# AdaLN block with attention and MLP on one core: fills moved to VectorE, one weight load moved to ScalarE's queue, the first quad planned by due time in pieces of two products

## The chip, the cores and the metric

The kernel runs on 1 core of one Trainium2 chip. The metric is device time in microseconds (us), median of several runs. One further execution was recorded by the hardware profiler; every row quoted below is from it. TensorE is written PE, its weight loads PEld, VectorE DVE, ScalarE ACT, GpSimd POOL, SyncE SP.

## The reference

All inputs are bf16. x is 2048 tokens by 512; there are 32 heads of 16; the MLP is 1376 wide.

```python
mod = (_silu(c) @ w_mod).reshape(c.shape[0], 6, 1, -1)
sa, ca, ga, sb, cb, gb = (mod[:, i] for i in range(6))
h = _layernorm(x) * (1 + ca) + sa
x = x + ga * attention(h, A_wqkv, A_wo)      # softmax(q k^T / 4) v, then wo
h = _layernorm(x) * (1 + cb) + sb
x = x + gb * (gelu(h @ B_w1 + B_b1) @ B_w2 + B_b2)
```

## The kernel before, in words

**Tiles.** The tokens are cut into 4 blocks of 512 (`xb[0..3]`). The normalized, modulated input is held transposed as `hT` (4 chunks of 128 features by 2048 tokens), the keys as `kT`, the values as `VE` (16 key tiles of 128, per head 16 values and two columns of ones, so that the product of weights and `VE` gives numerator and denominator in one). Attention goes by *quads*: one quad is 4 heads (one parity of one chunk of 128 features) for one block of 512 queries; there are 32 quads, each with 16 key tiles. An *item* is one head's scores for one key tile (128x512).

**Two ways to the exponential.** Most items go through ACT: `qk` writes 3 items into PSUM tile `sA`, then 2 into `sB`, in turn, and ACT writes `pA` or `pB` (L967). The key tiles in `DKT` (3, 7, 11, 15) are done by DVE instead: a pass per item turns the scores into int16 `t` whose bits read as f16 are the exponential (L1033, 4 passes for a key tile), and three shifts add a constant (L1054) to give copies that go with scaled values `VV`; four copies are accumulated (`NV = 4`). Quad 0 has no DVE tile in the kernel before, so it gives ACT 64 items and every other quad 48. `do_pv` accumulates into PSUM tile `od` (L1110); the copy `o_sb` (L1142) ends a quad.

**The front.** SP issues the loads in this order: `xb[0]` in four pieces, `W_m0` (1 MB, the modulation weights of the first layer norm), `W_k`, `xb[1]`, `W_q`, `W_v`, `xb[2]`, `xb[3]`, `W_m1`, `W_m2` and the eight pieces of `W_o_pad`. POOL fills `W_o_pad` with zeros (L145) and writes the ones columns of `VE` and `VV` (L142, L143, 56 small memsets). DVE takes the statistics of block 0 (L191), the silu of c (L177 to L179), the root by Newton steps (L196 to L210) and the norm (L216); PE computes the modulation (`psm`, L230), transposes (L221), and projects the first keys and queries (L266, L280); the evacuations are L261, L258, L272, L289 and L287.

**The planner.** From there on a planner in the kernel's Python text runs a clock with estimated durations and writes out a fixed order for each engine. Everything that is not attention is a `Job` with a due time `at` (measured in quads), a list of rows (engine, estimated duration, function), labels that it needs, and `hold`: up to that row it keeps one of two PSUM banks (tiles `aux`). The DVE passes take their scores through the same two banks. `job_for` gives an engine the first ready row of the list of active jobs, and then the first startable job. If PE has nothing ready, `do_fill` issues four products of zeros (L1131). The early jobs (norms, transposes `h_job`, `k_job`, `v_job` of blocks 1 to 3) stand sorted before all others, and until they are done and `end_early` has exchanged the banks, no DVE tile may start (`psd` is empty):

```python
        if not psd and all(o.at >= 0.9 for o in jobs) and not [o for o in active if o.hold >= 0]:
            if all(t + SEM <= clock for t in bank_rel):
                end_early()
```

A projection of four products (`proj_job`), an up-projection (`up_`) and half of an output projection (`oproj`) are one row of PE each, which nothing interrupts. `fill_stream` may hand a late DVE tile back to ACT.

After quad 31 `last_tail` does output projection and MLP of the last block, and `general_path` is a branch for inputs out of range that is not taken.

Of the kernel before, what the change touches and what calls it, by code (L numbers as in the profile page):

```python
# [20 lines left out]
P = 128  # L21
# [3 lines left out]
H = 32  # L25
# [31 lines left out]
EXP = {1: 0.5, 2: 0.92, 3: 1.34}  # L57

# [23 lines left out]
def adaln_block(ctx: ExitStack, tc: tile.TileContext, A_x, A_wqkv, A_wo, B_x, B_w1, B_b1, B_w2, B_b2,  # L82
# [41 lines left out]
    W_m0 = load_mod(0, nc.sync)  # L124
# [16 lines left out]
    def ve_ones(dst, v):  # L141
        nc.gpsimd.memset(dst[:, 0:H * HS].rearrange("p (h e) -> p h e", e=HS)[:, :, 16:HS], v)  # L142
        nc.gpsimd.memset(dst[:, H * HS:VEW], 0.0)  # L143

    nc.gpsimd.memset(W_o_pad, 0.0)  # L145
# [16 lines left out]
    for kt in range(NKT):  # L162
        ve_ones(VE[:, kt, :], 1.0)
    if ndk:
        for i in range(ndk):
            for j in range(1, NV):
                ve_ones(VV[:, i, j - 1, :], WJ[j])
# [25 lines left out]
    def ln_rstd(st, n):  # L193
        mv = small.tile([P, 12, 2], FP32, name="mv")
# [7 lines left out]
        nc.vector.tensor_tensor(out=ri[:, 0:n], in0=magic[:, 0:n], in1=ri[:, 0:n], op=ALU.subtract)  # L202
        r = ri[:, 0:n].bitcast(FP32)
# [30 lines left out]
    def mod_row(ps, W, col0):  # L234
        for j in range(NC):
            nc.tensor.matmul(out=ps, lhsT=scb[:, j, :], rhs=W[:, j, col0:col0 + D],
                             start=(j == 0), stop=(j == NC - 1))
# [26 lines left out]
    def k_proj(ps, ch, b):  # L264
        for j in range(NC):
            nc.tensor.matmul(out=ps, lhsT=W_k[:, j, ch * P:(ch + 1) * P], rhs=hT[:, j, b * 512:(b + 1) * 512],  # L266
                             start=(j == 0), stop=(j == NC - 1))
# [10 lines left out]
    def q_proj(ps, ch, b):  # L278
        for j in range(NC):
            nc.tensor.matmul(out=ps, lhsT=W_q[:, j, ch * P:(ch + 1) * P], rhs=hT[:, j, b * 512:(b + 1) * 512],  # L280
                             start=(j == 0), stop=(j == NC - 1))
# [11 lines left out]
    def v_proj(ps, kt):  # L293
        for j in range(NC):
            nc.tensor.matmul(out=ps, lhsT=hT[:, j, kt * P:(kt + 1) * P], rhs=W_v[:, j, :],  # L295
                             start=(j == 0), stop=(j == NC - 1))
# [33 lines left out]
    with tc.tile_pool(name="pps", bufs=1, space=PSUM) as pps0, \  # L330
# [3 lines left out]
        silu_c()  # L334
        psm = pps0.tile([P, 16], FP32, name="psm")
        first_mod_mm(psm)
        ln1_norm([0], st0)
# [15 lines left out]
    for r in range(4):  # L353
        for par in range(2):
            nc.sync.dma_start(out=W_o4[32 * r:32 * r + 16, :, par, :], in_=wo_v[r][:, :, par, :])
# [15 lines left out]
    early = ExitStack()  # L371
    banks = [early.enter_context(tc.tile_pool(name=f"psE{i}", bufs=1, space=PSUM)) for i in range(2)]
    psd = {}

    def end_early():
        early.close()
        psd["D"] = True
        banks[:] = [att.enter_context(tc.tile_pool(name=f"psX{i}", bufs=1, space=PSUM)) for i in range(2)]
# [26 lines left out]
    def ln_rows(b, src_of, dst_of, key):  # L405
# [3 lines left out]
        def rstd(j):  # L409
            st_of[b] = ln_rstd(st_of[b], 4)  # L410
        rows.append((DVE_, 2.2, rstd))
# [7 lines left out]
    def proj_job(at, mm, evac, needs, label, eng=DVE_, dur=V_EVAC, mms=4):  # L419
        def f(j):  # L420
            j.ps = j.alloc()
            mm(j.ps)

        def g(j):
            evac(j.ps)
        job(at, [(PE_, mms * MM, f), (eng, dur, g)], needs, label, 1)

    def v_job(at, kt):
        eng = V_ENG[kt]
        proj_job(at, lambda ps: v_proj(ps, kt), lambda ps: v_evac(ps, kt, eng), [("h", kt // 4)], ("v", kt),  # L430
                 ACT_ if eng == "act" else DVE_, 0.5 if eng == "act" else V_EVAC)

    def k_job(at, ch, b):
        proj_job(at, lambda ps: k_proj(ps, ch, b), lambda ps: k_evac(ps, ch, b), [("h", b)], ("k", ch, b))

    def q_job(at, ch, b, needs=()):
        proj_job(at, lambda ps: q_proj(ps, ch, b), lambda ps: q_evac(ps, ch, b), [("h", b), *needs],
# [14 lines left out]
    for b in range(1, NQB):  # L452
        at = 0.25 * (b - 1)
        if b > 1:
            def stats(j, b=b):
                st_of[b] = ln1([b])
            job(at - 0.16, [(DVE_, 2.5, stats)], [("n", b - 1)], ("st", b))
# [4 lines left out]
        if b == 1:  # L462
            for kt in range(4):
                v_job(-1.0, kt)
    for kt in range(4, NKT):
        v_job(0.25 * (kt // 4) + 0.04 * (kt % 4), kt)
    n_early = len(jobs)
    jobs.sort(key=lambda o: o.at)
    for i, kt in enumerate(DKT):
        def vv(j, kt=kt):  # L470
            vv_scale(kt)
        job(0.9 + 0.1 * i, [(DVE_, 0.9, vv)], [("v", kt)], ("vv", kt))
    for ch in range(1, NC):
        for b in range(NQB):
            k_job(1.0 + 2 * (ch - 1) * 0.9 + 0.2 * b, ch, b)
        q_job(1.7 + 2 * (ch - 1) * 0.9, ch, 0)

# [10 lines left out]
    def row_job(at, dst, W, col0, label):  # L488
        proj_job(at, lambda ps: mod_row(ps, W, col0), lambda ps: nc.vector.tensor_copy(out=dst, in_=ps),
# [43 lines left out]
    def tail_jobs(b):  # L533
# [15 lines left out]
        def oproj(tt):  # L549
            def f(half):  # L550
                def g(j):
                    if half == 0:
                        j.ps = j.alloc()
                    for t in range(4 * half, 4 * half + 4):
# [11 lines left out]
            def stats(j):  # L566
                ln_stats(T["x1"], T["st"], tt, tt)
            job(p0 + 0.5 + 0.25 * tt, [(PE_, 4 * MM, f(0)), (PE_, 4 * MM, f(1)), (DVE_, V_EVAC, mul),
                                       (POOL_, 1.2, res), (DVE_, V_EVAC, stats)],
                [("begin", b)] + [("ot", b, t) for t in range(8)] + ([("o", b, tt - 2)] if tt > 1 else []),  # L570
                ("o", b, tt), 2)
# [19 lines left out]
        def up_(fc):  # L591
            def f(j):
                j.ps = j.alloc()
                for c in range(NC):
                    nc.tensor.matmul(out=j.ps, lhsT=late["W_1"][:, c, fc * P:(fc + 1) * P], rhs=T["h2"][:, c, :],  # L595
                                     start=(c == 0), stop=(c == NC - 1))

            def g(j):
                nc.vector.tensor_scalar(out=T["u"][:, fc, :], in0=j.ps, scalar1=late["b1c"][:, fc:fc + 1],  # L599
                                        scalar2=None, op0=ALU.add)  # L600
            job(p0 + 2.3 + 0.2 * fc, [(PE_, 4 * MM, f), (DVE_, V_EVAC + 0.05, g)], [("h2", b, c) for c in range(NC)],
                ("u", b, fc), 1)
# [9 lines left out]
        def down(tt):  # L612
            def f(part):
                def g(j):
# [3 lines left out]
                    for fc in range(4 * part, min(NFC, 4 * part + 4)):  # L618
# [8 lines left out]
            def res(j):  # L627
# [3 lines left out]
            job(p0 + 4.9 + 0.5 * tt, [(PE_, 5 * MM, f(0)), (PE_, 4 * MM, f(1)), (PE_, 3 * MM, f(2)),  # L631
                                      (DVE_, V_EVAC, mul), (POOL_, 1.2, res)],
                [("g", b)] + [("y", b, tt - 1)] * (tt > 0), ("y", b, tt) if tt < 3 else ("tail", b), 3)
# [6 lines left out]
    jobs[n_early:] = sorted(jobs[n_early:], key=lambda o: o.at)  # L640
# [233 lines left out]
    def d_of(qi):  # L874
        return DKT if qi > 0 else ()
# [115 lines left out]
    def d_ready():  # L991
        if not psd or not d_tiles or len(d_items) == D_BANKS:
            return False
        if not any(seen_by(t) for t in bank_rel):
# [36 lines left out]
    def do_pass():  # L1031
# [5 lines left out]
        d_prog[0] = qi + (DKT.index(kt) + (4 - len(d_rows_left[(qi, kt)])) / 4) / len(DKT)  # L1037
# [148 lines left out]
    def start_ok(o, eng):  # L1186
        if o.at > progress() or o.rows[0][0] != eng or not all(has(x) for x in o.needs):
            return False
        if o.hold >= 0:
            if psd and any(a.hold >= 0 and a.i <= a.hold for a in active):  # L1190
# [4 lines left out]
    def job_for(eng):  # L1195

        for o in active:
            if o.rows[o.i][0] == eng:
                same = o.i and o.rows[o.i - 1][0] == eng
                if (o.same if same else o.other) <= clock + 1e-6:  # L1200
                    return o
        for o in jobs[:24]:
            if start_ok(o, eng):
                return o
        return None
# [85 lines left out]
    def dve_step():  # L1291
# [6 lines left out]
        if o is not None and (not psd or o.i or d_prog[0] > progress() + 0.1 or o.at + 0.4 < progress()  # L1298
# [28 lines left out]
    while pv["q"] < nq or od_copy or jobs or active:  # L1327
# [6 lines left out]
        if not psd and all(o.at >= 0.9 for o in jobs) and not [o for o in active if o.hold >= 0]:  # L1334
            if all(t + SEM <= clock for t in bank_rel):
                end_early()
                bank_rel[:] = [0.0, 0.0]
# [42 lines left out]
```

## Time and profile before

| | us |
|---|---|
| median of 3 runs | 849.57 (846.89, 849.81, 849.57) |
| the profiled execution, whole | 845.99 |
| its span (first to last instruction) | 844.2 |
| first exponential on ACT starts | 20.05 |
| copy of quad 0, of quad 1 (L1142) starts | 65.53, 99.16 |
| busy: PE, DVE, ACT, POOL | 789.4, 730.8, 755.5, 80.6 |

The page gives busy times per engine, the span in 40 slices, the chain of work that ended last, and groups of instructions by source line. Besides it a trace can be asked for the timeline of a stretch, for who waited for whom, and for the busy time of each engine in given windows. Rows of one line that follow each other are merged ("x4" is four instructions); in square brackets stands the idle time of the engine before the row and what ended it. PE's rows overlap since products are pipelined: the distance between starts counts, not the row's length. What is busy on an engine that others do not wait for costs nothing.

### The profile page before, as it was taken

Reading aid. Unit: us, or ns where it says so; the run is one execution under the profiler, and the core shown is the slowest. Engines: PE = TensorE matmul, PEld = TensorE weight load, DVE = VectorE, ACT = ScalarE, POOL = GpSimd, SP = SyncE. Lnnn points to the kernel's source line nnn. Section 1 sums busy time; section 2 is a strip of 40 time slices with the busy share of each in tenths; the row PEclk is TensorE's granted clock in tenths of the full one; section 3 lists DMA queues with packets and bytes.
Section 4 is the critical chain, followed back from the end, with each engine's and each line's share of the span. In section 5 each row is a group of like instructions: output and inputs, shape, how many; then the busy total and the mean of one; then the engine's idle time right before and its main releaser. Section 6 shows DMA issues by size and latency. Waiting matters only on the chain.

```text
span 844.2 us, 19140 instructions
## 1 busy us (share of the span) xinstructions
PE 789.4 (94%) x7859; PEld 253.0 (30%) x7921; DVE 730.8 (87%) x1306; ACT 755.5 (89%) x672; POOL 80.6 (10%) x125
## 2 busy tenths in 40 slices
PE   3999999999999999999999999999999999999967
PEld 2332322322223222222323223222223222322343
DVE  8747999999988999889989999889987999778573
ACT  2789799999999999999999999989998999999832
POOL 3000000000012000011011000011012000011010
PEclk9999999999999999999999999999999999999989
DMA  9200000004100000000100000000100000000000
GB/s 296 54 1 14 3 16 16 14 16 149 39 15 15 15 16 14 10 21 27 40 14 15 16 14 15 9 21 27 40 15 15 14 16 14 9 21 28 15 26 28
DMA packets 29631, 24.56 MB, mean 29 GB/s; under 512 B 13825, under 2 KB 23394, under 8 KB 29538
## 3 DMA queue, kind: packets, MB, share of 16 engines
q1 hardware_dynamic: 29010, 23.28, 9.4%
q8 instruction: 64, 1.05, 0.5%
q14 instruction: 29, 0.24, 0.1%
q10 hardware_dynamic: 528, 0.00, 0.0%
HBM read 20.65 MB, written 2.61 MB: 28 GB/s over the span
## 4 chain that ended last, share of the span: by engine, by line
PE 43%; DVE 29%; ACT 19%; issue 8%; POOL 1%; DMA 0%; SPq 0%; DVEq 0%; POOLq 0%; ACTq 0%
DVE t L1033 11%; PE od L1110 11%; ACT pA L967 10%; DVE t L1054 9%; ACT pB L967 6%; PE sA L915 5%; PE sB L915 5%; PE od L1131 3%; PE aux L915 3%; PE aux L619 3%; PE aux L595 2%; PE aux L555 2%; PE aux L295 2%; PE aux L266 1%; ACT uG L608 1%
## 5 line engine op out<-in xcount | busy, mean ns | idle before, releaser
L967 ACT ACTIVATE pA<-sA 128x1536 bf16<-128x1536 f32 (+1 forms) x311 | 464.0, 1492 | 25.4 <-PE sA L915 9.7
L967 ACT ACTIVATE pB<-sB 128x1024 bf16<-128x1024 f32 x310 | 330.6, 1067 | 10.3 <-PE aux L915 4.6
L1033 DVE TENSOR_SCALAR t<-aux 128x512 int16<-128x512 f32 x496 | 324.3, 681 | 14.0 <-PE aux L915 12.8
L1054 DVE TENSOR_SCALAR t<-t 128x2048 int16<-128x2048 int16 x372 | 263.9, 728 | 5.5 <-PE od L1110 4.6
L915 PE MATMUL aux<-qm,kT 32*128 32x512 bf16 x496 | 177.4, 380 | 5.7 <-DVE t L1033 4.3
L915 PEld LDWEIGHTS <-kT 32*128 32x128 bf16 x2048 | 77.7, 91 | 260.2 <-issue 254.6
L1110 PE MATMUL od<-pA,VE 128*32 128x512 bf16 x932 | 144.3, 385 | 0.1
L1110 PE MATMUL od<-pB,VE 128*32 128x512 bf16 x620 | 143.2, 385 | 1.0 <-DVE o_sb L1142 0.9
L1110 PE MATMUL od<-t,VV 128*32 128x512 f16 x1488 | 138.3, 384 | 2.5 <-DVE t L1054 2.3
L915 PE MATMUL sA<-qm,kT 32*128 32x512 bf16 x932 | 124.8, 383 | 9.8 <-ACT pA L967 6.7
L915 PE MATMUL sB<-qm,kT 32*128 32x512 bf16 x620 | 122.8, 384 | 1.6 <-ACT pB L967 0.9
L1131 PE MATMUL od<-hT,zeros 128*32 128x512 bf16 x1288 | 108.4, 383 | 0.0
L1167 POOL TENSOR_TENSOR OT<-o_sb,rb 128x512 bf16<-128x512 f32 x31 | 41.6, 1343 | 526.8 <-DMA rb<-d 262.7
L1110 PEld LDWEIGHTS <-VE 128*32 128x32 bf16 x2048 | 50.4, 94 | 101.6 <-issue 89.7
L1110 PEld LDWEIGHTS <-VV 128*32 128x32 bf16 x1488 | 41.0, 95 | 53.3 <-issue 41.4
L1110 PE MATMUL od<-t,VE 128*32 128x512 f16 x496 | 48.4, 384 | 1.0 <-DVE o_sb L1142 1.0
L1131 PEld LDWEIGHTS <-zeros 128*32 128x32 bf16 x1404 | 32.8, 95 | 53.0 <-issue 42.1
L595 PE MATMUL aux<-h2T,W 128*128 128x512 bf16 x114 | 32.9, 382 | 1.5 <-DVE uG L599 0.5
L619 PE MATMUL aux<-W,uG 128*128 128x512 bf16 x121 | 32.2, 387 | 1.7 <-issue 1.6
L1142 DVE COPY o_sb<-od 128x512 f32<-128x512 f32 x32 | 21.9, 685 | 12.2 <-issue 10.7
L599 DVE TENSOR_SCALAR uG<-aux,b1c 128x512 bf16<-128x512 f32 x33 | 24.6, 747 | 4.9 <-PE aux L595 4.7
L555 PE MATMUL aux<-W_o_pad,OT 128*128 128x512 bf16 x88 | 24.1, 382 | 0.6 <-issue 0.3
(126 smaller groups left out, 433.2 us busy)
## 6 DMA issues: line engine op xcount, KB each, us to landing
rb<-d SPq DMA_DIRECT2D x124, 64.0 KB
W_m<-in_w_mod_dram SPq DMA_DIRECT2D x3, 1024.0 KB
xr<-in_A_x_dram SPq DMA_DIRECT2D x4, 512.0 KB
out_dram<-ob SPq DMA_DIRECT2D x16, 128.0 KB
xb<-in_A_x_dram SPq DMA_DIRECT2D x3, 512.0 KB
W<-in_B_w_dram SPq DMA_DIRECT2D x1, 1376.0 KB
W<-in_B_w_dram SPq DMA_DIRECT2D x1, 1280.0 KB
xb<-in_A_x_dram SPq DMA_DIRECT2D x4, 128.0 KB
```

Source lines behind the costliest of these rows:

```text
L555: nc.tensor.matmul(out=j.ps, lhsT=OT[(b, t)][:, tt * P:(tt + 1) * P], rhs=W_o_pad[:, t, :], start=(t == 0), stop=(t == 7))
L595: nc.tensor.matmul(out=j.ps, lhsT=late["W_1"][:, c, fc * P:(fc + 1) * P], rhs=T["h2"][:, c, :], start=(c == 0), stop=(c == NC - 1))
L599: nc.vector.tensor_scalar(out=T["u"][:, fc, :], in0=j.ps, scalar1=late["b1c"][:, fc:fc + 1], scalar2=None, op0=ALU.add)
L619: nc.tensor.matmul(out=j.ps, lhsT=T["u"][:, fc, tt * P:(tt + 1) * P], rhs=late["W_2"][:, fc, :], start=False, stop=(fc == NFC - 1))
L915: nc.tensor.matmul(out=dst, lhsT=kT[32 * r:32 * r + 32, ch, kt * P:(kt + 1) * P], rhs=qm[(b, ch)][32 * r:32 * r + 32, par, :], start=True, ...
L967: nc.scalar.activation(out=pt[:, 0:n, :], in_=st[:, 0:n, :], func=ACT.Exp, scale=math.log(2.0) / STEP)
L1033: nc.vector.tensor_scalar(out=t0[(qi, kt)][:, r, :], in0=sd, scalar1=T_BIAS, scalar2=0.0, op0=ALU.add, op1=ALU.max)
L1054: nc.vector.tensor_scalar(out=t16, in0=t0[(qi, kt)], scalar1=float(MJ[j]), scalar2=None, op0=ALU.add)
L1110: nc.tensor.matmul(out=od[qi][32 * r:32 * r + 32, :], lhsT=w, rhs=src, start=first, stop=last_)
L1131: nc.tensor.matmul(out=dst[32 * r:32 * r + 32, :], lhsT=zeros, rhs=hT[:, r, 0:512], start=bank is not None, stop=bank is not None)
L1142: nc.vector.tensor_copy(out=o, in_=od[qi])
L1167: nc.gpsimd.tensor_tensor(out=OT[(b, t)], in0=o, in1=j.rb, op=ALU.mult)
```

## The change

- **Fills.** POOL's 56 memsets and its fill of `W_o_pad` go. DVE writes the ones columns of all of `VE` in two memsets and of `VV` in six; `warm` (128x512 zeros) is a ninth. `W_o_pad` is zeroed by DVE and loaded by SP in a job `load_wo` at 4.5 quads.
- **W_m0** is issued from ACT's queue, after `cc_bf`.
- **Warm-up.** PE does 18 products of zeros before the modulation and 4 after it.
- **Pieces of two products.** Projections, up, down and output projections are PE rows of two products; between two pieces other work may be issued while the job keeps its bank.
- **Planning of the first quad.** The separate early banks and the gate `psd` go. `job_for` takes the row with the smallest `at` among active and waiting jobs. Statistics become four rows, the root two; `v_job` times change. While progress is below 0.95, DVE takes jobs ahead of passes, and several jobs may hold banks; while it is below 1.0, a DVE tile's row needs both banks free.
- **One DVE tile in quad 0** (`DKT0 = (15,)`): it gives ACT 60 items, DVE 4 passes and 3 shifts.

```diff
+EARLY = 0.95
+D_ALONE = 1.0
+DKT0 = (15,)
...
-    W_m0 = load_mod(0, nc.sync)
+    W_m0 = load_mod(0, nc.scalar)
...
-    nc.gpsimd.memset(W_o_pad, 0.0)
...
-    for kt in range(NKT):
-        ve_ones(VE[:, kt, :], 1.0)
...
+    warm = prow.tile([P, 512], BF16, name="warm")
+    nc.vector.memset(warm, 0.0)
+
+    def ve_ones(dst, v):
+        nc.vector.memset(dst[:, :, 0:H * HS].rearrange("p k (h e) -> p k h e", e=HS)[:, :, :, 16:HS], v)
+        nc.vector.memset(dst[:, :, H * HS:VEW], 0.0)
+
+    ve_ones(VE, 1.0)
+    for j in range(1, NV):
+        ve_ones(VV[:, :, j - 1, :], WJ[j])
...
+        idle = ppsm.tile([P, 512], FP32, name="ppj")
+
+        def warm_up(n):
+            for _ in range(n):
+                nc.tensor.matmul(out=idle, lhsT=warm[:, 0:P], rhs=warm, start=True, stop=True)
+        warm_up(18)
         psm = pps0.tile([P, 16], FP32, name="psm")
         first_mod_mm(psm)
+        warm_up(4)
...
-    for r in range(4):
-        for par in range(2):
-            nc.sync.dma_start(out=W_o4[32 * r:32 * r + 16, :, par, :], in_=wo_v[r][:, :, par, :])
+    def load_wo(j):
+        nc.vector.memset(W_o_pad, 0.0)
+        for r in range(4):
+            for par in range(2):
+                nc.sync.dma_start(out=W_o4[32 * r:32 * r + 16, :, par, :], in_=wo_v[r][:, :, par, :])
...
-        job(at, [(PE_, mms * MM, f), (eng, dur, g)], needs, label, 1)
+        job(at, [(PE_, 2 * MM, f(0)), (PE_, 2 * MM, f(1)), (eng, dur, g)], needs, label, 2)
...
-            job(at - 0.16, [(DVE_, 2.5, stats)], [("n", b - 1)], ("st", b))
+            job(at - 0.16, [(DVE_, V_EVAC, lambda j, b=b, t=t, f=stats: f(j, b, t)) for t in range(4)],
+                [("n", b - 1)], ("st", b))
...
-                v_job(-1.0, kt)
+                v_job(0.02, kt)
     for kt in range(4, NKT):
-        v_job(0.25 * (kt // 4) + 0.04 * (kt % 4), kt)
+        v_job(0.25 * (kt // 4) - 0.1 + 0.04 * (kt % 4), kt)
...
-        job(0.9 + 0.1 * i, [(DVE_, 0.9, vv)], [("v", kt)], ("vv", kt))
+        job(0.9 + 0.02 * i, [(DVE_, 0.75, vv)], [("v", kt)], ("vv", kt))
...
+    job(4.5, [(DVE_, 2.2, load_wo)], (), "wo")
...
-        return DKT if qi > 0 else ()
+        return DKT if qi > 0 else DKT0
...
-        if not psd or not d_tiles or len(d_items) == D_BANKS:
+        if not d_tiles or len(d_items) == D_BANKS:
             return False
-        if not any(seen_by(t) for t in bank_rel):
+        if sum(seen_by(t) for t in bank_rel) < (2 if progress() < D_ALONE else 1):
             return False
...
-            if psd and any(a.hold >= 0 and a.i <= a.hold for a in active):
+            if progress() > EARLY and any(a.hold >= 0 and a.i <= a.hold for a in active):
...
+        best = None
         for o in active:
             if o.rows[o.i][0] == eng:
                 same = o.i and o.rows[o.i - 1][0] == eng
-                if (o.same if same else o.other) <= clock + 1e-6:
-                    return o
+                if (o.same if same else o.other) <= clock + 1e-6 and (best is None or o.at < best.at):
+                    best = o
         for o in jobs[:24]:
+            if best is not None and best.at <= o.at:
+                break
             if start_ok(o, eng):
                 return o
-        return None
+        return best
...
-        if o is not None and (not psd or o.i or d_prog[0] > progress() + 0.1 or o.at + 0.4 < progress()
+        if o is not None and (progress() <= EARLY or o.i or d_prog[0] > progress() + 0.1 or o.at + 0.4 < progress()
```

How the built kernels differ in their fixed orders: exponentials on ACT 621 before and 619 after (1552 and 1548 items), DVE passes 496 and 500, shifts 372 and 375, products of zeros in fills 1404 and 952, of which 128 and 48 lie between the start of quad 0 and that of quad 1. Jobs of the bank kind are 130 in both; other work stands inside 24 of them before and inside 84 after, in 71 and 252 groups.

In DVE's order after, two statistics of the next block stand between the transposes' evacuations instead of all four and its norm, and quad 0's passes follow the last value evacuations. Between the first query evacuation (L300 after) and the copy of quad 0 (L1168 after) stand 102 DVE instructions: 8 statistics, 12 norms, 12 evacuations of `hT`, 5 of `kT`, 5 of `VE`, 12 of `VV`, 6 passes, 3 shifts and 39 small ones of three roots. Up to the copy of quad 1 stand 41 more: 22 passes, 12 shifts, 4 of `qm`, 2 of `kT`, one reciprocal.

## Prediction

> **What bounds the kernel now.** I read the busy times in windows first, to see which stage loses time. The columns after the window are its length, then busy time and number of instructions of PE, PEld, DVE, ACT and POOL, then clock, DMA share and GB/s.
>
> ```profile
> 0.00:10.00 10.00, 0.00 (x0) 0.00 (x0) 8.42 (x13) 1.49 (x2) 7.97 (x64) 1.00 0.71 219
> 10.00:20.00 10.00, 6.75 (x58) 3.93 (x60) 8.35 (x34) 2.67 (x4) 0.00 (x0) 1.00 1.08 363
> 20.00:30.00 10.00, 9.79 (x92) 3.69 (x95) 9.41 (x36) 9.00 (x11) 0.00 (x0) 1.00 0.70 156
> 30.00:40.00 10.00, 9.39 (x109) 3.76 (x104) 6.33 (x19) 5.73 (x5) 0.00 (x0) 1.00 0.01 2
> 40.00:50.00 10.00, 9.24 (x80) 3.66 (x80) 5.03 (x15) 7.53 (x10) 0.00 (x0) 1.00 0.00 0
> 50.00:60.00 10.00, 9.89 (x56) 3.21 (x57) 3.37 (x7) 9.09 (x11) 0.00 (x0) 1.00 0.01 2
> ...
> 80.00:100.00 20.00, 19.59 (x213) 5.65 (x214) 19.95 (x34) 13.97 (x13) 0.00 (x0) 1.00 0.01 2
> ...
> 300.00:400.00 100.00, 96.08 (x959) 28.83 (x961) 93.19 (x152) 96.96 (x82) 10.06 (x8) 1.00 0.06 18
> ```
>
> From 100 us on ACT is 96 to 97% busy: ACT's exponentials are the bound there, with DVE close behind (91 to 93%) and PE's rows padded with fills. Between the first exponential (20.05) and 100, ACT is idle for 1.00 + 4.27 + 2.47 + 0.91 + 0.03 (60 to 80) + 6.03 = 14.7 us, and DVE is half empty from 30 to 60 and full from 80. So there are two places to win: the 20 us before ACT starts and these 14.7.
>
> The front is read in the timeline of 0 to 40 us (start, length, engine, line).
>
> ```profile
> 2.00 6.61 DVE L155 TENSOR_SCALAR qmask<-pmask 128x2 f32<-128x2 f32 x1
> ...
> 3.30 5.38 DVE L191 BATCH_NORM_STATS2 st<-xb 128x6 f32<-128x512 bf16 x2
> ...
> 8.60 1.29 DVE L191 BATCH_NORM_STATS2 st<-xb 128x6 f32<-128x512 bf16 x2
> ...
> 10.16 0.10 PEld L230 LDWEIGHTS <-W_m 128*128 128x128 bf16 x1 [10.16 <-DMA W_m<-in_w_mod_dram]
> ...
> 15.29 1.91 PE L266 MATMUL ppj<-hT,W_k 128*128 128x512 bf16 x4
> ...
> 18.68 0.75 DVE L289 TENSOR_SCALAR qm<-ppj,qmask 128x512 bf16<-128x512 f32 x1 [0.65 <-PE ppj L280]
> ...
> 20.53 1.90 PE L295 MATMUL aux<-W_v,hT 128*128 128x512 bf16 x8
> ```
>
> A two-column operation on DVE takes 6.61 us and ends at 8.61, just as POOL's memsets end (the last starts at 8.48); two statistics take 5.38 where later four take 2.46. DVE stands while POOL fills, and the chain of waits names L155. The four products of L266 take 1.91 us, the eight of L295 take 1.90: PE runs at half speed until some time between 18 and 20.5.
>
> The waits of ACT between 20 and 100 us tell the rest (total, times, longest).
>
> ```profile
> ACT pA L967 <- PE sA L915: 5.3, 2, 5.1
> ACT pA L967 <- PE aux L915: 3.1, 1, 3.1
> ACT VE L302 <- PE aux L295: 2.6, 3, 1.4
> ```
>
> The 5.1 is at 29 to 34 us, where the keys of block 1 are not ready; the 3.1 at 85 to 88, before quad 2's first scores, whose queries (L289, 86.32) stood behind late DVE tiles.
>
> **The change part by part.** The sum is made against the profiled execution, 845.99 us (span 844.2 and 1.8 around it). That is 3.6 below the median and 0.9 below the lowest timed run; I carry the result to the median by +2.
>
> *Fills and start.* Removed from DVE's way: 6.6 - 0.15 (a small operation, L151) = 6.4 us of standing. Added on DVE: nine memsets, 2272 elements a partition. Two memset rows of the trace, 0.165 us for 128 elements (L161) and 0.072 for 16 (L159), give 0.83 ns an element and 0.06 each: 2.4 us. Bounds are 0.33 ns (L1054, 2048 elements in 0.68 us) and 1.34 (L274, 512 in 0.69): 0.8 to 3.6. So statistics may start at 2.2 + 0.3 + 2.4 = 4.9 and end at 7.4, against 9.89. They also need `xb[0]`, which now shares the DMA engines with `W_m0`. Summing the GB/s of 1 us windows, 1.5 MB (both) had moved by 8.0 us; with that as the worst landing the statistics end at 8.7. I take 7.9, a gain of 2.0 (1.2 to 2.5). `W_m0` itself is wanted at 10.7 and was there at 10.16; the same bytes bound it. After it W_q is needed at about 14.6; its 3.1 MB had moved by 12.7. No gain is booked for the load's own move.
>
> A rule that speaks against that move is in the Trainium skill, "DMA: Bandwidth & Descriptors", on arbitration and on issuing engines: loads from different queues run on the same 16 engines, which serve the queues in turn, so a second queue saves only issue time. The row that bears on it is W_m0's issue on SP, 0.43 us at 2.62; by the rule the move is worth 0.4 us at most and puts the statistics at the worst landing, 8.7 instead of 7.9, and the sum's gain would be 0.8 lower.
>
> *Warm PE.* 18 products from 2.8 us take 7.7 at 0.43 (half speed) and 3.9 at 0.22 (L295, warm), so they end between 6.7 and 10.5. The modulation's input is ready at 10.4 - 2.0 = 8.4, the transposes' at 12.95 - 2.0 = 10.9; modulation (1.0) and four products (0.9) lie between, so only the worst end delays the path, by some 1.5 us, which the bounds below hold. In the path, the second half of the transposes and eight projection products fall from 0.43 to 0.22: after the last evacuation of `hT`, queries were ready 18.68 - 16.31 = 2.4 us later, and now about 1.5; transposes give 0.3. But DVE's order keeps block 1's four statistics (2.46) ahead of the query evacuation: 13.4 + 2.46 = 15.9 instead of 18.68 gives 2.8 at best. I take 2.5 for the first exponential: 17.5 (bounds 1.2 and 3.5).
>
> "TensorE: Matmul & The Clock Gate", on the clock gate, puts the change to full speed after about 3.4 us of activity. Here PE was still slow at 17.9, 4.9 us after its first transpose at 12.96, while the clock column reads 1.00 throughout. By the rule the 18 products end at 8.4, by the row at 9.2, and the sum is the same.
>
> *First stage, 14.7 us of idle ACT.* (a) The 5.1: norms of block 1 ended at 22.92 and its keys (L274) at 33.65, 10.7 later, because all statistics, the root and the norms of block 2 stood between. By the new order that interval holds four statistics (2.46), four evacuations (2.2), the two halves of the root (2.2), one norm (0.4) and the key evacuation (0.69): 8.0. Left of the 5.1: 2.4. (b) 2.5 us at 40 to 46 while values wait: a block then takes DVE 8.3 and ACT 16 x 0.49 + 4 x 0.58 = 10.2, so DVE is ahead; left 0.5. (c) The 6.0 at 80 to 100: DVE tiles began only at 74.4, quad 1's copy came at 99.16, when ACT had had its items since 85 and its buffers were full. In the new order DVE has from the first query evacuation (16.6) to the copy of quad 0: 8 x 0.62 + 3 x 2.2 + 12 x 0.345 + 12 x 0.52 + 10 x 0.69 + 12 x 0.23 + 6 x 0.64 + 3 x 0.65 = 37.3, so 54 at the earliest, and 27.0 more to that of quad 1. ACT has 17.5 + 60 x 0.49 + 11 x 0.58 = 53.3 for quad 0 and 23.5 more. With a few us of waits the copies come at about 59 and 86, and ACT is not held by full buffers; left 1.0. With 1.0 of small waits, 5.0 of 14.7 stay: gain 9.7 (4 to 12).
>
> *One DVE tile.* ACT has 4 items less: one `pA` and one `pB` size of work, 2.0 us. DVE gets 4 x 0.64 + 3 x 0.65 = 4.5 us, inside the stage where it had 20 us to spare. If that cover is gone it costs those 4.5.
>
> *Pieces of two.* A change of product kind costs PE 0.1 us (four products start at 63.78, the next scores at 64.75: 0.97 for 4 x 0.216). Counting kinds in the two orders gives 1312 and 1366 changes: 5.4 us on PE, against 113 groups of fills (24 us) that the order drops. PE is not the bound from 100 on; ACT's idle time there, 25.5 us, is put down to scores waited for, 9.2 of it behind products in `od` (L1110). Booked: 0 (a gain of 8 to a loss of 8).
>
> *The rest.* `load_wo`: a memset of 2048 words, 1.8 us at the price above (0.7 to 2.8), on a DVE 92% busy, and eight issues on SP, which took 12.2 us in the front while they waited for other loads; behind them stand quad 4's two copies of the denominators, whose product POOL needs only for a projection four quads later. 0 (loss up to 2). The tail is the same list: 0.
>
> Sum: 2.5 + 9.7 + 2.0 = 14.2, so 831.8 for a profiled execution, and 834 for the median.
>
> **The rivals.**
>
> *The gain is lost by quad 1 (846).* DVE waited for PE 21.8 us between 20 and 100 (7.0 for keys, 6.6 for `hT`, 5.7 for values). If DVE's new order, now 64 us long to quad 1's copy, keeps these waits, that copy comes at 16.6 + 37.3 + 27.0 + 21.8 = 103, not before 99, and the stall at 85 to 100 stays. Then the 2.0 us of items remain: 846.0 - 2.0 + 2. For: queues are in order, and PE was 93 to 99% busy there. Against: that includes 32 groups of fills, and 12 remain.
>
> *Banks held longer (860, slower).* A job now keeps one of two banks while others' work stands between its pieces: 252 groups instead of 71, 181 more of about 0.32 us = 58 us. With one bank, a DVE row goes scores, pass, scores at 1.2 us instead of 0.64, so about 45%, 26 us, of DVE time is lost. DVE was idle 69 us between 100 and 800, and already waited 12.0 for L915. If shifts can't fill these holes all of it comes: 834 + 26. It makes the kernel slower once some 20 of the 26 come through. Against: of a tile's 4.5 us, 2.0 are shifts, which need no bank and can trade places with passes, and the fills fell, so the order found work for PE.
>
> *Pieces help everywhere (826).* Scores come between pieces sooner, and a third of the 25.5 us goes too. For: 7.6 us of waits behind L1110 in five long ones. Against: these are not projections.
>
> **How the numbers follow.** Forecast 834: 0.70, with own range 826 to 842 (the terms' bounds taken together, not all at one end). Lost by quad 1: 0.12, half of it within 0.5% of 849.57, that is above 845.3, which is about what a measurement of this kernel can tell. Banks: 0.08. Pieces: 0.10. Faster 0.70 + 0.10 + 0.04 = 0.84, same 0.07, slower 0.09. The range 823 to 848 leaves out the banks and the outer ends of the others.
>
> **What would show it.** Right: POOL empty after 1.5 us, L156 at 0.15 us, statistics ended by 8, first exponential near 17.5, quad 1's copy near 86, ACT idle 5 us between its start and 100, and 96 to 97% after. Wrong: `xb[0]` late behind W_m0; a wait of over 4 us of ACT on scores before 60; quad 1's copy after 95; passes (L1059) waiting for scores by much more than 12 us after 100; ACT below 95% there.

## The result, and the profile after

| | before | changed |
|---|---|---|
| median of 4 runs, us | 848.23 (845.76 to 849.81) | 826.69 (826.67 to 827.04) |
| the profiled execution, whole | 845.99 | 827.04 |
| its span | 844.2 | 825.3 |
| first exponential starts | 20.05 | 20.42 |
| copy of quad 0, of quad 1 starts | 65.53, 99.16 | 65.25, 93.95 |
| last exponential ends | 798.23 | 779.02 |
| exponentials after quad 1's copy | 569 in 699.1, 1.229 each | 568 in 685.1, 1.206 each |
| ACT idle, 20 to 100 and 100 to 750 | 14.7, 23.1 | 10.7, 13.7 |

The ratio is 0.975, with a 95% interval of 0.9721 to 0.9778: the change takes about 21 us away. The forecast was 834 with a range of 823 to 848, and the time lies in it. But the table shows another sum than the one forecast. The front gained nothing, the first stage 5 us, and the largest part, 13 us, came after quad 1's copy, where nothing had been booked: 568 exponentials at 1.229 - 1.206. (One fall of PE's clock, of the kind described in the last section, lies in that stretch in the profile before, at 564 us, and none after; at the price found in experiment 5 that is about 1 us of the 13.)

The front in the timeline of the changed kernel (start, length, engine, line):

```profile
2.00 0.17 DVE L156 TENSOR_SCALAR qmask<-pmask 128x2 f32<-128x2 f32 x1
...
2.77 0.91 DVE L167 MEMSET VE<- 128x1024 bf16 x1 [0.16 <-issue]
...
4.69 1.24 DVE L196 BATCH_NORM_STATS2 st<-xb 128x6 f32<-128x512 bf16 x2
7.61 0.69 DVE L196 BATCH_NORM_STATS2 st<-xb 128x6 f32<-128x512 bf16 x1 [1.68 <-DMA xb<-in_A_x_dram]
...
9.84 0.69 DVE L196 BATCH_NORM_STATS2 st<-xb 128x6 f32<-128x512 bf16 x1 [1.54 <-DMA xb<-in_A_x_dram]
...
11.07 0.97 PE L241 MATMUL psm<-sc_bf,W_m 128*128 128x1 bf16 x32 [1.69 <-DVE sc_bf L184]
...
15.93 1.91 PE L277 MATMUL ppj<-hT,W_k 128*128 128x512 bf16 x4
...
20.42 1.44 ACT L993 ACTIVATE pA<-sA 128x1536 bf16<-128x1536 f32 x1
```

The small operation on the masks shrank from 6.61 us to 0.17, and DVE was ready for the statistics at 4.69. Then it waited twice for pieces of `xb[0]` and ended the fourth statistic at 10.5, later than before (9.9). The four products of L277 again take 1.91 us, so PE was at half speed in spite of its warm-up.

The busy times in windows, in the columns of the table shown for the kernel before:

```profile
10.00:20.00 10.00, 7.74 (x62) 4.11 (x63) 8.65 (x34) 2.31 (x4) 0.00 (x0) 0.66 1.08 361
20.00:30.00 10.00, 9.60 (x79) 4.01 (x77) 8.97 (x36) 9.35 (x11) 0.00 (x0) 1.00 0.21 77
30.00:40.00 10.00, 9.70 (x76) 3.71 (x74) 8.59 (x29) 8.93 (x10) 0.00 (x0) 1.00 0.01 2
40.00:50.00 10.00, 9.44 (x66) 3.76 (x67) 4.92 (x10) 8.80 (x9) 0.00 (x0) 1.00 0.00 0
50.00:60.00 10.00, 9.86 (x71) 2.73 (x71) 6.96 (x19) 8.69 (x10) 0.00 (x0) 1.00 0.01 2
...
80.00:100.00 20.00, 19.84 (x233) 5.55 (x225) 19.45 (x34) 13.94 (x13) 0.00 (x0) 1.00 0.01 2
...
300.00:400.00 100.00, 97.42 (x953) 28.11 (x960) 93.51 (x154) 99.06 (x84) 11.73 (x9) 1.00 0.09 26
```

ACT's 5.73 of 30 to 40 became 8.93, its 6 us of idling at 80 to 100 stayed, and 300 to 400 rose from 96.96 to 99.06. The waits of ACT between 20 and 100 (total, times, longest) say which is which. `pB <- od` means that the exponential into `pB` waited for a product into `od`:

```profile
ACT pB L993 <- PE od L1136: 5.1, 1, 5.1
ACT pB L993 <- PE sB L941: 2.7, 2, 1.4
ACT VE L313 <- PE aux L306: 2.7, 3, 1.4
```

The wait for the keys of block 1 is gone. The one long wait left is for `od`: ACT stands from 90 to 95 with its buffers full, until DVE has ended quad 1 (copy at 93.95).

The waits of ACT from 100 to 750 in the kernel before, of which the forecast had taken only those behind `od` apart:

```profile
ACT pA L967 <- PE od L1110: 7.6, 5, 2.8
ACT pB L967 <- PE aux L915: 4.6, 10, 2.2
ACT pA L967 <- PE sA L915: 4.4, 15, 0.5
ACT pA L967 <- PE aux L915: 2.9, 7, 0.9
ACT pB L967 <- PE sB L915: 2.0, 6, 0.7
```

And in the changed kernel:

```profile
ACT pA L993 <- PE od L1136: 5.4, 3, 3.0
ACT pA L993 <- PE sA L941: 2.3, 6, 0.6
ACT pB L993 <- PE aux L941: 1.8, 3, 0.9
ACT pA L993 <- PE aux L941: 1.1, 3, 0.6
```

Every kind of wait for scores (`sA`, `sB`, and `aux`, which is put here with them, since scores come behind those products in PE's order) fell: before 4.6 + 4.4 + 2.9 + 2.0 = 13.9 us in 38 waits, after 5.8 in 14 (with a last 0.6 for `sB`). This is many short waits, not one long one.

### The profile page after: what moved, and what is told of

It is laid out like the page before. It is cut to its first block, busy times and chain, and to the rows that moved or that the text cites. A ratio compares the mean times of both kernels' runs of the same rounds, so it can differ in the third digit from the quotient of the medians.

```text
span 825.3 us, 18246 instructions
## 1 busy us (share of the span) xinstructions
PE 774.9 (94%) x7438; PEld 239.6 (29%) x7503; DVE 732.9 (89%) x1323; ACT 750.4 (91%) x670; POOL 75.2 (9%) x68
## 4 chain that ended last, share of the span: by engine, by line
PE 42%; ACT 30%; DVE 16%; issue 10%; DMA 2%; SPq 0%; POOL 0%; ACTq 0%; DVEq 0%; POOLq 0%
ACT pA L993 16%; PE od L1136 12%; ACT pB L993 11%; DVE t L1059 6%; PE sA L941 6%; DVE t L1080 5%; PE sB L941 5%; PE aux L645 3%; PE aux L941 3%; PE aux L578 2%; ACT uG L634 2%; PE fb L719 1%; PE od L1157 1%; PE aux L620 1%; PE fb L728 1%
## 5 line engine op out<-in xcount | busy, mean ns | idle before, releaser
L993 ACT ACTIVATE pA<-sA 128x1536 bf16<-128x1536 f32 x310 | 469.3, 1514 | 10.3 <-PE od L1136 5.4
L1059 DVE TENSOR_SCALAR t<-aux 128x512 int16<-128x512 f32 x500 | 327.8, 679 | 29.2 <-PE aux L941 27.5
L993 ACT ACTIVATE pB<-sB 128x1024 bf16<-128x1024 f32 x309 | 337.0, 1091 | 11.3 <-PE od L1136 6.1
L1157 PE MATMUL od<-hT,zeros 128*32 128x512 bf16 x920 | 80.8, 383 | 0.0
L620 PE MATMUL aux<-h2T,W 128*128 128x512 bf16 x114 | 36.0, 385 | 0.8 <-DVE t L1059 0.7
L645 PE MATMUL aux<-W,uG 128*128 128x512 bf16 x119 | 34.9, 383 | 1.8 <-issue 1.7
L1157 PEld LDWEIGHTS <-zeros 128*32 128x32 bf16 x952 | 23.3, 95 | 36.4 <-issue 29.2
L1168 DVE COPY o_sb<-od 128x512 f32<-128x512 f32 x32 | 21.8, 682 | 8.7 <-issue 8.5
```

The lines of the kernel that those rows point to most:

```text
L645: nc.tensor.matmul(out=j.ps, lhsT=T["u"][:, fc, tt * P:(tt + 1) * P], rhs=late["W_2"][:, fc, :], start=False, stop=(fc == NFC - 1))
L993: nc.scalar.activation(out=pt[:, 0:n, :], in_=st[:, 0:n, :], func=ACT.Exp, scale=math.log(2.0) / STEP)
L1059: nc.vector.tensor_scalar(out=t0[(qi, kt)][:, r, :], in0=sd, scalar1=T_BIAS, scalar2=0.0, op0=ALU.add, op1=ALU.max)
L1157: nc.tensor.matmul(out=dst[32 * r:32 * r + 32, :], lhsT=zeros, rhs=hT[:, r, 0:512], start=bank is not None, stop=bank is not None)
L1168: nc.vector.tensor_copy(out=o, in_=od[qi])
```

## The experiments

Experiments 2 and 6 edit the kernel before, all others the changed kernel. All ratios are against the kernel before on the same chip (medians 848.40 for experiments 1, 2, 4 and 7, 847.14 for 6 and 8 to 10, 848.98 for 3, 5, 11 and 12). Times of different groups come from different chips, and one or two microseconds between them say little.

**1. The changed kernel without the pieces.** Theory A: pieces of two let scores between, and that is the gain after 100. Rival: the new planning is.

```diff
-        job(at, [(PE_, 2 * MM, f(0)), (PE_, 2 * MM, f(1)), (eng, dur, g)], needs, label, 2)
+        job(at, [(PE_, 4 * MM, both), (eng, dur, g)], needs, label, 1)
```

Up and output projections are likewise rows of 4 products, down projections of 5, 4 and 3.

> The changed kernel with its PE rows whole again: projections and up-projections are one row of four products, output projections two of four, down-projections 5, 4 and 3; all else as changed. From the first exponential's start on, the changed kernel gained 5.2 us up to quad 1's copy and 14 after it. Theory A (pieces of two give the later gain, since scores come between them): about 839 us (836 to 843), an exponential every 1.228 us after quad 1's copy instead of 1.206. Theory B (the plan by due time and the earlier start of DVE tiles give it): 825 to 830, 1.206 us kept.

Measured: 839.50 us, ratio 0.9882 (0.9836 to 0.9927). After quad 1's copy 569 exponentials took 701.3 us, 1.233 each: the rate of the kernel before (1.229). ACT waited for `sA` 8.4 us in 23 waits and behind `aux` 10.6. (A fall of the clock of twice the usual length, at 556 us, is in this profile: about 2.4 us at the price of experiment 5.)

Before that copy the pieces did the opposite. It came at 89.82 here, against 93.95 in the changed kernel; 23.9 us passed between the copies of quads 0 and 1, against 28.7; and of ACT's stand of 5.1 us for `od` between 20 and 100 us this is left:

```profile
ACT pA L999 <- PE od L1142: 1.2, 1, 1.2
```

So the late quad 1 of the changed kernel comes with its pieces; what in the order makes it late was not looked into.

**2. The old kernel with the pieces alone.**

```diff
-        job(at, [(PE_, mms * MM, f), (eng, dur, g)], needs, label, 1)
+        job(at, [(PE_, 2 * MM, f(0)), (PE_, 2 * MM, f(1)), (eng, dur, g)], needs, label, 2)
```

Up, down and output projections likewise; fills, loads and the first quad stay as they were.

> The kernel before with nothing but the pieces of two products. Theory A: about 836 us (832 to 840), the gain after quad 1's copy comes and the stage before it stays as it was. Theory B: 846 to 850. The forecast's slower rival (banks held longer): over 850.

Measured: 838.67, ratio 0.9893 (0.9846 to 0.9940). 569 exponentials in 691.5 us, 1.215 each. The stage before did not stay as it was: quad 1's copy came at 95.49, 3.7 us earlier. (The profiled run, 834.40, is the fastest of the four.) The busy times from 100 to 750 (window, length, PE, PEld, DVE, ACT, POOL, clock, DMA share, GB/s), first of the changed kernel without pieces, then of the old one with them:

```profile
100.00:750.00 650.00, 628.29 (x6374) 190.66 (x6423) 599.06 (x1010) 626.25 (x536) 66.40 (x54) 0.99 0.08 23
```

```profile
100.00:750.00 650.00, 620.99 (x6196) 181.11 (x6251) 602.78 (x1025) 635.30 (x546) 69.15 (x55) 1.00 0.08 23
```

And of the kernel before, then of the changed one:

```profile
100.00:750.00 650.00, 625.72 (x6380) 190.95 (x6434) 598.86 (x1016) 626.94 (x537) 63.04 (x53) 1.00 0.08 22
```

```profile
100.00:750.00 650.00, 621.93 (x6155) 180.57 (x6205) 607.59 (x1030) 636.32 (x548) 67.18 (x55) 1.00 0.09 24
```

ACT is the fourth pair of numbers: 626.25 and 635.30 stand beside 626.94 before and 636.32 after. All four cases agree: with pieces of two ACT works 8 to 10 us more in this stretch, without them it doesn't, whatever the planning of the first quad. By the medians the two halves bring 8.9 (new front and first quad) and 9.7 (pieces), each give or take some 4, against about 21 for both.

**3. Where in the work the pieces count: only output, up and down projections in pieces,** q, k and v projections whole.

```diff
-        job(at, [(PE_, 2 * MM, f(0)), (PE_, 2 * MM, f(1)), (eng, dur, g)], needs, label, 2)
+        job(at, [(PE_, 4 * MM, both), (eng, dur, g)], needs, label, 1)
```

> The changed kernel with projections (keys, queries, values and the gate rows) whole again and only output, up- and down-projections in pieces of two. W_m0 stays on ACT's queue. If the gain goes by the products that are split (264 of the MLP's and output's after quad 7 against 108 of projections from quad 1 on): 830 to 833, two thirds of the way from whole (839.5) to the changed kernel (826.7). Rival (projections that hold up the next quad count most): 835 to 839.

Measured: 831.14, ratio 0.9806 (0.9763 to 0.9849), as expected, and 1.219 an exponential after quad 1's copy. By the medians (839.50, 831.14, 826.69) two thirds of the gain come from the jobs that run through the whole kernel and a third from the projections. By the rate after quad 1's copy (1.233, 1.219, 1.206) it is half and half, but there the projections' pieces have also cost something before: with projections whole, 24.4 us pass between the copies of quads 0 and 1 and ACT waits 1.2 us at most for `od`, as in experiment 1.

**4. W_m0 back on SP's queue.** Theory: `xb[0]` waits because W_m0 shares the engines. Rival: `xb[0]` would have landed late anyhow.

```diff
-    W_m0 = load_mod(0, nc.scalar)
+    W_m0 = load_mod(0, nc.sync)
```

> The changed kernel with W_m0 issued by SP after xb[0], as before. In the changed kernel DVE waited 1.7 and 1.5 us for the last two pieces of xb[0]. Theory C (sharing the DMA engines with W_m0 is what made them late, and it cost the front its gain): statistics end near 7.5 us, the first exponential starts at 17.5 to 18.3 instead of 20.4, time 824 to 825. Rival (the pieces come late for another reason, or W_m0's own landing then holds the chain): the first exponential stays at 19.8 to 20.6, time 826 to 828.

Measured: 824.98, ratio 0.9723 (0.9683 to 0.9763). From its timeline of the front:

```profile
4.70 2.42 DVE L196 BATCH_NORM_STATS2 st<-xb 128x6 f32<-128x512 bf16 x4
...
10.02 0.95 PE L241 MATMUL psm<-sc_bf,W_m 128*128 128x1 bf16 x32 [1.89 <-DMA W_m<-in_w_mod_dram]
...
12.94 0.83 PE L277 MATMUL ppj<-hT,W_k 128*128 128x512 bf16 x3
...
16.98 1.44 ACT L993 ACTIVATE pA<-sA 128x1536 bf16<-128x1536 f32 x1
```

Four statistics without a wait, ended at 7.1 instead of 10.5. W_m0 came at 10.02; from ACT's queue its first piece of work was released at 9.66. The move had brought W_m0 0.4 us and cost the statistics, which wait for `xb[0]`, 3.4, and the first exponential 3.4 (20.42 against 16.98). The theory holds; the size differs from profile to profile. In the five profiles with the new front and W_m0 on ACT's queue (changed kernel, experiments 1, 3, 7 and 9) the statistics end at 9.67 to 10.54 and the first exponential starts at 19.32 to 20.42; in the six with it on SP's queue (4, 5, 8, 10, 11, 12) they end at 6.85 to 7.13 and it starts at 16.98 to 17.78.

**5. The same kernel again,** since the median had moved by only 1.7 us.

> The changed kernel with W_m0 on SP once more, on the same chip as the three others, to compare with them: 823 to 826 us, first exponential at 16.8 to 17.3.

Measured: 825.50, ratio 0.9720 (0.9687 to 0.9753), first exponential at 17.00. The medians of the two rounds, 824.98 and 825.50, lie below the changed kernel's 826.69, but the intervals overlap. What happened to the 3.4 us can be followed by exponential in the profiled executions. The changed kernel is 3.44 us behind that of experiment 4 at the first exponential, 3.35 behind at the 101st, 2.4 at the 301st and 3.1 at the end: the head start stays. The repeat, the same program, keeps within 0.3 us of its twin for 200 exponentials, and then loses 1.2 near 262 us and 1.4 near 573, at two places where the granted clock falls (last section); a further 0.9 between 630 and 690 us comes without a fall. Its best runs were 823.3 and 824.0, those of the changed kernel 826.7. So, exponential by exponential, one load on the other queue is worth about 3 us. By the medians it is 1.2 to 1.7, which the intervals don't separate from nothing. This version has the lowest medians of the study, together with experiment 8.

**6. The fills alone in the old kernel** (DVE memsets and `load_wo` at 4.5, W_m0 on SP).

```diff
-    nc.gpsimd.memset(W_o_pad, 0.0)
...
+    ve_ones(VE, 1.0)
...
+    job(4.5, [(DVE_, 2.2, load_wo)], (), "wo")
```

> The kernel before with nothing but the fills moved from POOL to DVE (and W_o_pad zeroed and loaded at 4.5 quads). W_m0 stays on SP, PE is not warmed. Theory C (POOL's memsets held DVE, and only W_m0's queue hid that gain in the changed kernel): statistics end near 7.2 us, the first exponential starts at 18.0 to 18.9 instead of 20.05; the time falls by 1 to 2 us, to 846 to 848, since block 1's wait stays. Rival (xb[0] comes late anyway): first exponential at 19.5 to 20.5, no change.

Measured: 842.71, ratio 0.9941 (0.9920 to 0.9962): 4.4 us, more than either theory expected. The statistics start at 4.42, the first exponential at 17.21 instead of 20.05, quad 1's copy at 96.29 instead of 99.16. The 2.85 us of the front pass on whole; why the median gained 1.6 more stays open.

**7. and 8. Without the warm-up** (its products and its memset), once with W_m0 on ACT's queue, once on SP's.

```diff
-        warm_up(18)
...
-        warm_up(4)
```

> The changed kernel without the 22 warm-up products and their memset. In the changed kernel the four products of the key projection still took 1.91 us, so the warmth had gone. Theory D (the warm-up is lost in the 1.7 us for which PE then waits): first exponential within 0.4 us of 20.4, time 826 to 828. Rival (part of it is kept): 828 to 830.

> The changed kernel with W_m0 on SP and without the warm-up products. With W_m0 on SP and the warm-up, the last three steps ran at full speed (products 0.22 us apart) and the first exponential started at 16.98. Theory D (the warm-up is worth something once its warmth is not lost in a wait): first exponential at 17.8 to 18.6, time 1 to 1.5 us above the kernel with W_m0 on SP. Rival: the four statistics ahead of the query evacuation hide it, first exponential within 0.3 us of 16.98.

Measured: 827.66, ratio 0.9738 (0.9698 to 0.9778), and 825.18, ratio 0.9746 (0.9699 to 0.9793). First exponential at 19.32 and 17.11, against 20.42 and 16.98 with warm-up. No gain of the warm-up shows in either median. That the first of the two starts 1.1 us earlier without it was not expected; 19.32 lies at the end of the spread given in experiment 4. With W_m0 on SP the query weights land at 14.9 and the four statistics of block 1 (2.47 us from 13.1) hold the query evacuation, so slow products are hidden.

**9. and 10. Is ACT's stand at 90 to 95 worth 5 us?** Theory: DVE ends quad 1 late, and one tile less before that point takes the stand away and gives up to 5.1 us back, less the items that ACT gets (two exponentials more). Rival: ACT had run ahead, and the time comes back elsewhere. One kernel gives quad 0 no DVE tile, the other (W_m0 on SP) gives quad 1 three instead of four.

```diff
-DKT0 = (15,)
+DKT0 = ()
```

> The changed kernel with no DVE tile in quad 0 (64 items on ACT there, DVE tiles from quad 1 on). By the forecast's term the tile is worth its 4 items, 2.0 us: 828 to 829. Rival 1: DVE is the late engine at the copy of quad 1 (93.95, ACT waits 5.1 us before it), so a tile less frees 4.5 us of DVE and the stall shrinks: 824 to 826. Rival 2: DVE idles meanwhile, and nothing is gained or lost but the items.

```diff
-        return DKT if qi > 0 else DKT0
+        return DKT if qi > 1 else DKT[1:] if qi else DKT0
```

> The changed kernel with W_m0 on SP, and quad 1 with three DVE tiles instead of four. ACT waits 5.1 us before quad 1's copy for buffers that the late DVE tiles keep full. Theory E (DVE's lateness in quad 1 is the stall's cause): the wait falls to under 2 us; ACT has 4 items more (2.0 us); time 1 to 3 us below W_m0 on SP alone, 822 to 824. Rival (the lateness moves to quad 2): the wait comes back there, and the time rises by the items, 826 to 827.

Measured: 827.59, ratio 0.9767 (0.9719 to 0.9814), and 828.04, ratio 0.9774 (0.9728 to 0.9819). From the waits of ACT between 20 and 100 in the second:

```profile
ACT VE L313 <- PE aux L306: 2.5, 2, 1.4
ACT pB L993 <- PE sB L941: 1.3, 1, 1.3
...
ACT pA L993 <- PE od L1136: 0.3, 1, 0.3
```

The stand is gone (5.1 to 0.3), quad 1's copy came at 85.19 instead of 90.51, and yet the kernel is not faster than its twin (824.98), and slower than either theory expected. ACT's idle time fell from 10.5 to 6.0 us in 20 to 100 and rose from 13.8 to 18.1 in 100 to 750: it was given back later. Part of that is due to falls of the clock in this profile, one at 86 us and one at 455, some 1.2 us each by the price of experiment 5. The first kernel has none after 20 us, like the changed kernel: its last exponential ends 1.3 us later than the changed kernel's, with two exponentials more (2.4 at 1.206). So, by these two profiles, the stand was worth about one us of its 5.1.

**11. Two DVE tiles in quad 0** (W_m0 on SP).

```diff
-DKT0 = (15,)
+DKT0 = (11, 15)
```

> The changed kernel with W_m0 on SP and two DVE tiles in quad 0 (11 and 15): ACT 1545 items instead of 1548. If ACT's items count alone (theory F, after three tiles in quad 1 cost 3 us and none in quad 0 about 1): 1 to 2 us below W_m0 on SP alone, 823 to 824. Rival: DVE, full from 80 us on, falls further behind and hands its tiles' lateness on: 826 to 830.

Measured: 826.63, ratio 0.9743 (0.9713 to 0.9772), 618 exponentials, quad 0's copy at 68.62 instead of 61.82. No gain, as the rival says: the last exponential ends 2.6 us after that of experiment 4.

**12. Pieces of one product** (W_m0 on SP). Theory A continued: shorter still lets scores in sooner. Rival: banks held longer starve DVE, as the slow rival of the forecast says.

```diff
-        job(at, [(PE_, 2 * MM, f(0)), (PE_, 2 * MM, f(1)), (eng, dur, g)], needs, label, 2)
+        job(at, [(PE_, MM, f(i)) for i in range(4)] + [(eng, dur, g)], needs, label, 4)
```

Up, down and output projections likewise.

> The changed kernel with W_m0 on SP and PE rows of one product each. Theory A taken further (what counts is how long a job keeps scores out of PE; four products cost 0.97 us, two 0.53, one 0.32): the step from four to two gave 13 us, that from two to one would give 3 to 6, 819 to 822. Rival (each change of product kind costs 0.1 us, there are 126 more of them, and banks are held through 374 interposed groups instead of 252): no gain or a loss, 825 to 832.

Measured: 844.81, ratio 0.9954 (0.9935 to 0.9972): far above what theory and rival expected. Nearly the whole gain is lost again, and an exponential after quad 1's copy takes 1.245. DVE's waits from 100 to 750 with pieces of one:

```profile
DVE t L1059 <- PE aux L941: 36.4, 53, 1.7
DVE uG L625 <- PE aux L620: 6.3, 7, 1.2
DVE rp L1185 <- DMA dall<-d: 5.1, 1, 5.1
```

And the same in the changed kernel, where pieces are of two:

```profile
DVE t L1059 <- PE aux L941: 22.4, 38, 1.6
```

ACT's waits with pieces of one:

```profile
ACT pA L993 <- PE od L1136: 16.2, 7, 9.2
ACT pA L993 <- PE sA L941: 6.8, 5, 5.1
```

DVE's passes stand 14 us more for scores (12 more than the 24.6 of experiment 4, the twin with pieces of two), and DVE works 586.4 us of these 650 instead of 607.6. ACT's short waits for scores are few, but it now stands 9.2 us at 511 to 520 for `od`: DVE is full there, PE fills its time largely with products of zeros, and the quad's DVE tiles end the stand. The 5.1 for `sA` ends at 196.5, just after DVE's wait of 5.1 for a copy of the denominators ended at 194.5, in the window in which the late weights are loaded.

Followed by exponential against experiment 4, the loss is not spread evenly. The kernel is 0.3 us behind at 158 us, 9.5 at 204, 10.2 at 507, 19.5 at 521 and 22.6 at the end. The first step holds the wait for the denominators (5.2 us) and two falls of the clock (159 and 193 us), the second is the stand at 511 to 520. That the bank is held longer is what the edit does; that it causes these two steps is not shown.

## Why the prediction was right, and where its steps failed

The number held by luck, by errors that cancel: of the 2.5 booked in the front nothing came, of the 9.7 in the first stage 4.0 (14.7 to 10.7 of ACT's idle time), and 13 came where 0 was booked.

- **Fills: right, as far as they go.** L156 took 0.17 (0.15 forecast). The nine memsets lie between 2.33 and 4.7, 2.4 us as summed (0.91 for 1024 elements, 0.27 for 256), and DVE was free at 4.7 (4.9 forecast).
- **First exponential 17.5: wrong (20.42).** The failing term is the landing of `xb[0]` behind W_m0. The worst landing had been set at 8.0 us, by summing bytes; the last piece came at about 9.8. The text had named this as the sign of an error, and the rule of the Trainium skill, "DMA: Bandwidth & Descriptors" (issuing engines are not separate DMA queues), spoke against the move; experiment 4 agrees with it: 0.4 us for W_m0 (0.4 at most by the rule), 3.4 lost by the statistics. By the rule the gain was to be 0.8 lower; it was lower by the whole 2.5 and more. With W_m0 on SP the first exponential came at 16.98. The warm-up, part of the same 2.5, gave nothing that shows: 17.11 without it.
- **(a) the keys of block 1: 5.1 to 2.4 forecast, 5.1 to nothing measured.** Better than summed.
- **(b) 2.5 to 0.5 forecast: wrong.** ACT idles 1.2 and 1.3 in 40 to 50 and 50 to 60; 2.7 us of waits for values (L306) stay.
- **(c) 6.0 to 1.0 forecast: wrong.** Quad 1's copy came at 93.95, not 86, and the stand at `od` stayed. Between the copies of quads 0 and 1 passed 28.7 us where 27.0 were summed; it was quad 0's, summed to 59, that came 6 late, at 65.25, and 2.9 of these 6 are the late front. The rest is DVE's waits for PE: from the first query evacuation to the copy of quad 0 DVE was idle 10.9 us (18.2 before), above all for values (4.6), `hT` (2.8) and keys (1.9), where about 5 had been allowed (its work, 35.3, was 2 less than summed). With the front mended (experiment 4) the copies came at 61.82 and 90.51. With the projections whole (experiments 1 and 3) 23.9 and 24.4 us pass between the copies and the stand is gone: in the new planning the pieces, booked at 0, lengthened this stage. Experiments 9 and 10 add what the step had not asked: ACT had run ahead here, and the stand was worth about one of its 5 us. To count all idle time of the bounding engine as loss was the wrong price.
- **DVE tile, 2.0:** experiment 9, without it, ends 1.3 us later; not far off.
- **Pieces of two, booked 0 (8 to -8): the largest mistake, 13 us.** The step looked at PE's cost of changing between kinds and at the 9.2 us of ACT behind `od`. The row that mattered is the wait for scores, 13.9 us in 38 waits of which none is over 2.2. The rival "pieces help everywhere" had the mechanism right and its size too small (8.5, a third of the idle time); that its 826 meets the measured time is luck too, since it took the forecast's 14.2 for the rest.
- **Banks held longer:** not at two products, and at one product experiment 12 shows a loss, of which held banks may be a part. The sign given for it, passes that wait much more than 12 us after 100, did come (10.3 to 22.4) while the kernel got faster: DVE had room for it (607.6 of 650). It was a bad sign for an engine with slack.
- **`load_wo` and the tail, 0:** last exponential to end took 47.8 us before and 48.0 after.

The forecast chance of 0.10 for pieces and of 0.12 for a stall that stays at quad 1 were both claims about single terms. In its term the first came true; of the second, the stall did (5.1 us), though not its copy at 103. They went in opposite directions.

## What to carry to other kernels

Where one engine feeds the bound engine and also does side work, look at how long a piece of side work keeps it, and count the bound engine's many short waits: halving pieces from four products to two took 13 us away here, and pieces of one product gave it back, most of it in two places of 9 us each. The second DMA queue brought a large load 0.4 us and made a small one some 3 us late: before a large load is moved forward, ask which small load is needed first. Price an idle stretch by what is late because of it: here an engine that had run ahead stood for 5 us and lost about one, while a stand of 9.2 us in experiment 12 cost all of it.

## What the runs showed of the hardware

**The clock also fell where PE had waited for only 0.95 us, and not in every run.** In the repeat of experiment 4 PE waits 0.95 us for `sA` at 263.11, and its next rows are longer (0.51 and 0.61 instead of 0.39). The timeline of PE there:

```profile
261.76 0.39 PE L941 MATMUL sB<-qm,kT 32*128 32x512 bf16 x2 [0.19 <-ACT pB L993]
263.11 0.51 PE L941 MATMUL sA<-qm,kT 32*128 32x512 bf16 x3 [0.95 <-ACT pA L993]
263.55 0.61 PE L1136 MATMUL od<-pA,VE 128*32 128x512 bf16 x1
```

The same place in experiment 4, the same program:

```profile
263.38 0.39 PE L941 MATMUL sA<-qm,kT 32*128 32x512 bf16 x3 [0.95 <-ACT pA L993]
263.70 0.39 PE L1136 MATMUL od<-pA,VE 128*32 128x512 bf16 x1
```

The same wait, and no fall; near 573 us it is so again, with 0.95 in both. In windows of one us of the repeat (the clock is the number after POOL's):

```profile
262.00:263.00 1.00, 0.15 (x2) 0.00 (x0) 0.95 (x4) 1.00 (x2) 0.00 (x0) 1.00 0.00 0
263.00:264.00 1.00, 0.89 (x11) 0.28 (x14) 1.00 (x4) 1.00 (x3) 0.00 (x0) 0.63 0.00 0
264.00:265.00 1.00, 1.00 (x16) 0.27 (x8) 1.00 (x3) 1.00 (x1) 0.00 (x0) 0.50 0.03 8
265.00:266.00 1.00, 1.00 (x14) 0.19 (x6) 1.00 (x2) 0.32 (x1) 0.00 (x0) 0.50 0.08 8
266.00:267.00 1.00, 1.00 (x11) 0.43 (x12) 0.08 (x2) 0.92 (x1) 0.00 (x0) 0.67 0.00 0
```

Summed, (0.37 + 0.50 + 0.50 + 0.33) x 2 = 3.4 us at half speed, and ACT lost 1.2. The Trainium skill, "TensorE: Matmul & The Clock Gate", on the clock gate, gives the two states and a window of 3.4 us that runs freely, which agrees with the length. It asks for such a window of idling before the clock falls; here 0.95 us of waiting stood before it. That the wait is the cause is not shown: the same wait in experiment 4 was followed by no fall.

The front too differs between two profiles. Between its 18 products and the next ones PE had 2.9 us with only the 32 short products of L241, in the changed kernel and in experiment 4 alike. In the first the clock column reads 0.66 between 10 and 20 us, that is 6.8 us at half speed, two such windows; in the second it reads 1.00. (Before the first change on record the column tells nothing: it reads 1.00 from 0 to 10 us too, where the rows show products 0.43 us apart.) The 18 products took 6.72 and 5.46 us. At 0.43 slow and 0.22 warm the second makes 3.2 us of slow work, near the page's 3.4, and the first 5.7, which is more than one such window. So medians of a few runs can differ by as much as such falls, and variants 1 or 2 us apart were compared above by exponential, with the falls of each profile beside them.
